# A linear-attention block and two expert layers on one core: a new order of the first four chunks, six early weight halves on TensorE, and later scores

## The chip, the core and the metric

The kernel runs on one core of a Trainium2 chip. The core has five engines that run side by side, each in the order of its own instruction stream: TensorE (PE; its weight loads are shown apart as PEld), VectorE (DVE), ScalarE (ACT), GpSimd (POOL) and SyncE (SP), which here only issues transfers (DMA). SBUF is the on-chip memory, PSUM the memory that TensorE writes its sums to, and HBM the large memory that inputs, outputs and scratch lie in. The metric is device time in microseconds (us) of one execution, from its start to its end.

## The reference, cut

A complex-valued linear recurrence over 768 time steps (4 batches, 8 heads, 48 by 48 states), then a mixture of four experts, then one wide layer with a leaky ReLU:

```python
def _attn_ref(q, k, v, a_re, a_im):
    ...
    for t in range(S):
        new_re = ar * S_re - ai * S_im
        new_im = ar * S_im + ai * S_re
        kv = np.einsum('bhd,bhe->bhde', k[:, :, t], v[:, :, t])
        S_re, S_im = (new_re + kv, new_im)
        y[:, :, t] = np.einsum('bhd,bhde->bhe', q[:, :, t], S_re)

def _moe_ref(x, domain_probs, w1, w2):
    ...
    for e in range(E):
        h = np.maximum(x @ w1[e], 0.0)
        out += p[:, e:e + 1] * (h @ w2[e])

def _moe2_ref(x, w_in, w_out):
    h = x @ w_in
    g = np.maximum(0.01 * h, h)
    return (g @ w_out).astype(np.float32)
```

## The kernel before, in words

The 3072 tokens are cut into 24 chunks of 128, and four chunks make a group of 512. For each chunk there are two pieces of work, both written as generators that are advanced one step (one `yield`) at a time.

`elementwise(c)` turns the four planes of a chunk (real and imaginary decay, q and k) into features. It takes logarithms, exponentials, an arctangent and sines on ACT, running sums and products on DVE (the scans at L202, L207 and L219), range reduction of the phase (L222 to L228), and at last the features `ft` (L243). POOL multiplies q and k by the decay (L208, L215).

`products(c)` does the attention of the chunk. `by_head` (L253) rearranges `ft` into `hd` by six transfers. TensorE transposes the keys (`pt`, L279; ACT copies them to `kt`), forms the scores (`sc`, L292; DVE masks them to `att`), the new state (`pm`, L303) and the output (`py`, L315 and L317; ACT copies it to `y`), and transposes that (`px`, L325). ACT and DVE split `px` into a high part `xh` (L333) and a low part `xl` (L334). These are the inputs of the expert layers. The scores and the output read `hd`; the transposes read only `ft`.

The experts and the wide layer are cut into units of 128 hidden columns, 32 and 16 per group. A unit is nine matmuls of 512 columns into `ph` (L442), a step on DVE and ACT that gives `hp`, `hh` and `hl`, and nine matmuls into the accumulators (L471 to L473). Products run three times, on high and low parts. In group 0 the first eight units are done in halves of 256 columns: first for chunks 0 and 1, then for chunks 2 and 3. In group 0 each expert weight is loaded raw (`load_unit`), split by ACT and POOL into two parts (`split_unit`, L418 and L419), and stored to a scratch in HBM (L608); later uses load the split form (`load_split`, L410). The weights of the wide layer come as 64-bit numbers and are decoded by `decode` from unit 33 on, a third of a half unit at a time (L358 to L368), and stored too (L372).

The order is written out by hand. Ahead of the unit loop the string `PLAN` names what is advanced next: digits are `elementwise` of chunks 0 to 3, the letters p, q, r and t are `products` of chunks 0 to 3, n the probabilities, s one half of a weight to be split. `warm` (L161) adds matmuls that compute nothing that is used. After that `tick` advances one background generator, up to three steps at each of two places per unit, so that a number of steps is done by a given unit (`pace`, L557). For chunks from 4 on, each round of the background has `NSTEPS` steps: those in `PSTEPS` go to `products(c)`, the rest to `elementwise(c + 1)`. With the old table `by_head` is step 1, the transposes are 3 and 5, the scores 8 and 10, the state 13, the output 16 and 18, `px` 21. `load_chunk(c + 2)` stands at the start of the round (L532).

SP issues nearly all transfers in the order of the program, so a transfer that waits holds back those behind it. That matters for three of them: the six `hd` transfers (L261), the loads of chunks (L148, L152), and the loads of raw 64-bit weights (L342), whose buffer is one of three.

Of the kernel before, what the change touches and what calls it, by code (L numbers as in the profile page):

```python
# [20 lines left out]
P = 128  # L21
# [14 lines left out]
WARM = 1, 2, 3, 0  # L36
PLAN = "0100100111100n10s1s0s100s1s0s00110s22113p2q1332p322q32p2p3q2p3q3q2q3p23pq2pq223333"
# [3 lines left out]
FTK = (1,)  # L41
# [7 lines left out]
PSTEPS = (1, 3, 5, 8, 10, 13, 16, 18, 21)  # L49
ESTEPS = 16  # L50
NSTEPS = ESTEPS + len(PSTEPS)
WAIT = 4
HDG = (1,)
# [8 lines left out]
def fused_kernel(  # L62
# [20 lines left out]
    with ExitStack() as fast:  # L83
# [26 lines left out]
        G.memset(ones, 1.0)  # L110
        zero_b = const.tile([P, 1], F32, name="zero_b")
# [49 lines left out]
        def warm(x, n):  # L161

            out = ps_acc.tile([P, TG], F32, name="warm", tag="acc0")
            for _ in range(n):
                PE.matmul(out[:, : NG * P], ident, x.rearrange("p g t -> p (g t)"), start=True, stop=True)

        def elementwise(c):
# [22 lines left out]
            act(r, r, AF.Exp, scale=-1.0)  # L190
# [4 lines left out]
            act(a, a, AF.Ln)  # L195
            S.tensor_tensor(r, en, r, ALU.mult)
            yield
            act(b, a, AF.Exp, scale=-0.5, bias=ln_b)
# [10 lines left out]
            act(a, b, AF.Exp, scale=-0.5)  # L209
# [3 lines left out]
            V.scalar_tensor_tensor(b, en, -1.0, a, ALU.mult, ALU.mult)  # L213
            V.scalar_tensor_tensor(a, b, 2.0, a, ALU.add, ALU.mult)
# [5 lines left out]
            if c >= CPG:  # L220
                yield
# [3 lines left out]
            if c >= CPG:  # L225
                yield
# [3 lines left out]
            if c == 0:  # L230
                warm(th, WARM[0])
# [7 lines left out]
            if c == 1:  # L239
                warm(th, WARM[1])  # L240
            yield
            for i, x in ((0, q), (1, k)):
                (G if i and c in FTK else V).tensor_tensor(  # L243
                    ft[:, :, :, i * P : (i + 1) * P], cs,
                    x[:, None].to_broadcast([P, 2, NG, P]), ALU.mult,
                )
                if i or c >= CPG:
                    yield
# [4 lines left out]
        def by_head(c):  # L253
# [14 lines left out]
        def products(c):  # L268
# [16 lines left out]
            if c < 2:  # L285
                warm(last_phase[c], WARM[2])
# [10 lines left out]
            if c < 2:  # L297
                warm(last_phase[c], WARM[3])
# [49 lines left out]

        def decode(i):
# [18 lines left out]
            G.tensor_tensor(wt[:, 1], wo, wt[:, 0].bitcast(F32), ALU.subtract)  # L368
            yield
            load_raw64(i + 3)  # L370
            if stored:
                SP.dma_start(*stored.pop())  # L372
            stored.append((ws[NU1 + u][:, half], wt.bitcast(F32)))
# [38 lines left out]
        def split_unit(s, part):  # L412
            if s >= len(order) or not fresh[s]:
# [5 lines left out]
            G.tensor_tensor(wt[:, 1], raw, wt[:, 0].bitcast(F32), ALU.subtract)  # L419
            if part:  # L420
# [68 lines left out]
        with tc.manual_schedule():  # L489
# [13 lines left out]
            splits = iter([(0, 0), (0, 1), (1, 0), (1, 1), (2, 0), (2, 1), (3, 0)])  # L503
            for x in PLAN + "0" * 14 + "1" * 14 + "pq" * 8 + "s" * 7:
# [5 lines left out]
                elif x == "s":  # L510
                    for s, part in islice(splits, 1):
                        split_unit(s, part)
                        if part and s < 2:
                            load_unit(s + 5)

            def background():
                for _ in zipped(steps["2"], steps["3"]):
# [307 lines left out]
```

## Time and profile before

| what | value |
|---|---|
| median of 3 runs | 1506.38 us (1501.48 to 2019.27) |
| profiled execution | 1506.07 us, of which its span is 1504.2 us |
| TensorE busy | 1403.8 us, 93% of the span |
| VectorE, ScalarE, GpSimd busy | 864.8, 566.7, 263.6 us |
| chain that ended last | PE 60%, DVE 8%, DMA 3%, ACT 2%, issue 2% |
| HBM | 203 GB/s over the span |

Busy time is the time in which an engine had an instruction under way. "PEclk" is the share of full speed that TensorE's clock was granted in a stretch. It has two levels, 2.4 and 1.2 GHz, so 0.5 is the lower one and a value between them a mix. The number in square brackets behind a row of the timeline is how long the engine stood idle before it, and what released it.

### The profile page before, as it was taken

The numbers are of one execution on the slowest core, as the hardware profiler recorded it, in microseconds if no ns is written. First come the engines' busy times: TensorE is split into PE (matmuls) and PEld (weight loads), VectorE is DVE, ScalarE is ACT, GpSimd is POOL, SyncE is SP. The second block draws the span as 40 slices with busy tenths as digits, with TensorE's granted clock in tenths as the row PEclk, the third lists the DMA queues.
The fourth block names the chain that finished last, engine by engine and source line by source line (L and its number), as shares of the span: only waits on it lengthen the run. The fifth ranks groups of instructions, "written<-read, shape, count | busy, mean of one in ns | idle before, by whom it ended". The sixth has DMA issues, their size and how long they took to land.

```text
span 1504.2 us, 18506 instructions
## 1 busy us (share of the span) xinstructions
PE 1403.8 (93%) x6972; PEld 1177.8 (78%) x6972; DVE 864.8 (57%) x1503; ACT 566.7 (38%) x957; POOL 263.6 (18%) x251
## 2 busy tenths in 40 slices
PE   1888888999899989999999999999999999999997
PEld 0787667888777878878888888888888888888886
DVE  8838566669787878876455555455443333333332
ACT  5535455533444344355333354333242111323232
POOL 5113455311223122121001021001010000100000
PEclk9789989999999999999999999999999999999999
DMA  5498776887788698776776575676565655556562
GB/s 194 53 321 262 243 224 210 246 290 241 236 271 259 248 286 254 264 243 192 236 226 195 195 229 170 232 226 171 178 200 175 218 202 204 193 189 210 190 210 65
DMA packets 91042, 325.48 MB, mean 216 GB/s; under 512 B 10464, under 2 KB 32064, under 8 KB 90944
## 3 DMA queue, kind: packets, MB, share of 16 engines
q1 hardware_dynamic: 88064, 319.24, 66.8%
q10 hardware_dynamic: 2880, 4.98, 1.0%
q8 instruction: 56, 0.92, 0.3%
q14 instruction: 42, 0.34, 0.1%
HBM read 262.72 MB, written 42.52 MB: 203 GB/s over the span
## 4 chain that ended last, share of the span: by engine, by line
PE 60%; DVE 8%; DMA 3%; ACT 2%; issue 2%; POOL 0%; SPq 0%; DVEq 0%; ACTq 0%; POOLq 0%
PE ph L442 27%; PE acc L471 9%; PE acc L473 9%; PE acc L472 9%; DVE hl L460 2%; PE sc L292 1%; PE py L315 1%; PE py L317 1%; DMA vt<-in_v_dram 1%; DVE hp L447 1%; ACT hh L459 1%; DMA ws_scratch<-dw 1%; PE pm L303 1%; DVE ft L243 1%; DMA r<-in_w_dram 1%
## 5 line engine op out<-in xcount | busy, mean ns | idle before, releaser
L442 PE MATMUL ph<-xh,wt 128*128 128x512 f32 (+1 forms) x1200 | 407.5, 396 | 6.9 <-DMA wt<-ws_scratch 6.3
L471 PE MATMUL acc<-hh,wt 128*128 128x512 f32 (+1 forms) x888 | 350.0, 394 | 6.9 <-ACT o L586 6.9
L473 PE MATMUL acc<-hl,wt 128*128 128x512 f32 (+1 forms) x888 | 341.9, 385 | 0.0
L472 PE MATMUL acc<-hh,wt 128*128 128x512 f32 (+1 forms) x888 | 341.2, 384 | 0.0
L459 ACT CAST hh<-hp 128x512 fp32r<-128x512 f32 (+1 forms) x296 | 180.6, 610 | 402.1 <-DVE hp L447 315.4
L460 DVE TENSOR_TENSOR hl<-hp,hh 128x512 fp32r<-128x512 f32 (+1 forms) x296 | 213.5, 721 | 183.6 <-ACT hh L459 183.1
L442 PEld LDWEIGHTS ph<-xh,wt 128*128 128x128 f32 x1200 | 231.4, 195 | 51.8 <-DMA wt<-ws_scratch 7.4
L447 DVE SCALAR_TENSOR_TENSOR hp<-ph,pb 128x512 f32<-128x512 f32 (+1 forms) x200 | 133.4, 667 | 199.9 <-PE ph L442 199.8
L442 PE MATMUL ph<-xl,wt 128*128 128x512 f32 (+1 forms) x600 | 234.5, 391 | 1.1 <-DVE xl L334 1.1
L442 PE MATMUL ph<-x2h,wt 128*128 128x512 f32 x576 | 198.0, 398 | 0.0
L471 PEld LDWEIGHTS acc<-hh,wt 128*128 128x128 f32 x888 | 167.5, 189 | 38.2 <-ACT o L586 7.6
L473 PEld LDWEIGHTS acc<-hl,wt 128*128 128x128 f32 x888 | 167.1, 188 | 34.1
L472 PEld LDWEIGHTS acc<-hh,wt 128*128 128x128 f32 x888 | 167.7, 189 | 31.0
L450 DVE SCALAR_TENSOR_TENSOR hp<-hp 128x512 f32<-128x512 f32 x96 | 72.3, 753 | 171.7 <-ACT hp L449 171.7
L442 PEld LDWEIGHTS ph<-xl,wt 128*128 128x128 f32 x600 | 117.4, 196 | 22.0 <-DVE xl L334 1.6
L442 PEld LDWEIGHTS ph<-x2h,wt 128*128 128x128 f32 x576 | 108.7, 189 | 25.2
L449 ACT COPY hp<-ph 128x512 f32<-128x512 f32 x96 | 56.3, 586 | 168.0 <-PE ph L442 168.0
L442 PE MATMUL ph<-x2l,wt 128*128 128x512 f32 x288 | 114.5, 397 | 0.0
L292 PE MATMUL sc<-hd 96*128 96x128 f32 x384 | 58.3, 302 | 35.8 <-DMA hd<-ft 26.7
L292 PEld LDWEIGHTS sc<-hd 96*128 96x128 f32 x384 | 55.7, 215 | 42.8 <-issue 22.7
L419 POOL TENSOR_TENSOR wt<-raw,wt 128x384 fp32r<-128x384 f32 x64 | 71.9, 1144 | 57.2 <-ACT wt L418 56.9
L208 POOL TENSOR_TENSOR aaqk<-aaqk,ge 128x384 f32<-128x384 f32 x24 | 26.5, 1103 | 252.1 <-DVE ge L207 252.1
(94 smaller groups left out, 1467.2 us busy)
## 6 DMA issues: line engine op xcount, KB each, us to landing
wt<-ws_scratch SPq DMA_DIRECT2D x264, 768.0 KB, 4.8
ws_scratch<-wt SPq DMA_DIRECT2D x32, 768.0 KB, 8.1
hd<-ft SPq DMA_DIRECT2D x142, 128.5 KB, 7.2
aaqk<-in_attn_dram SPq DMA_DIRECT2D x22, 768.0 KB, 5.8
raw<-in_w_dram SPq DMA_DIRECT2D x32, 384.0 KB, 4.1
r<-in_w_dram SPq DMA_DIRECT2D x32, 384.0 KB, 3.8
ws_scratch<-dw SPq DMA_DIRECT2D x32, 384.0 KB, 4.2
pb<-pn_scratch SPq DMA_DIRECT2D x24, 256.0 KB, 6.5
```

The lines of the kernel that those rows point to most:

```text
L208: G.tensor_tensor(q, q, en, ALU.mult)
L292: PE.matmul(sc[:, j], hd[:, h, P : 2 * P], hd[:, h, :P], start=True, stop=True)
L419: G.tensor_tensor(wt[:, 1], raw, wt[:, 0].bitcast(F32), ALU.subtract)
L442: PE.matmul(ph[:, : t1 - t0], wt[:, wi, cols], x[kc][:, t0:t1], start=n == 0, stop=n == 3 * NG - 1)
L447: V.scalar_tensor_tensor(hp, ph, 0.0, pbs[g, u // 8][:, t0:t1], ALU.max, ALU.mult)
L449: A.copy(hp, ph)
L450: V.scalar_tensor_tensor(hp, hp, 0.01, hp, ALU.mult, ALU.max)
L459: A.copy(hh, hp)
L460: V.tensor_tensor(hl, hp, hh.bitcast(F32), ALU.subtract)
L471: PE.matmul(out, wt[:, 0, cols], hh, start=first, stop=False)
L472: PE.matmul(out, wt[:, 1, cols], hh, start=False, stop=False)
L473: PE.matmul(out, wt[:, 0, cols], hl, start=False, stop=last)
```

## The change

It has five parts.

1. **Order of the start.** A new `PLAN` finishes the features of chunks 0 and 1, then their products, and takes chunks 2 and 3 only eight steps far ahead of the unit loop (14 before), the rest in the background. The `warm` matmuls go. The features of chunk 1 are all made by DVE (POOL made half of them). Three of the six `hd` transfers of chunks 0 and 1 are issued by ACT.
2. **Early weight halves.** Six halves are split by a new way: ACT casts the high part (`cast_early`), TensorE forms the rest as raw minus high in PSUM with the identity and its negative, and ACT copies it out (`rest_early`). POOL has no part in it.
3. **Steps of `elementwise`.** ACT takes the square first and the exponential of r later; one exponential goes to `g` in place of `a`; there are 17 steps for all chunks.
4. **Later scores.** The scores move from steps 8 and 10 to 12 and 14 of a round, what follows moves by four steps or three, and `load_chunk(c + 2)` moves from the start of the round to step 9.
5. **Decoding.** The store of the decoded half is issued ahead of the next raw load, and that load goes to the buffer freed one half earlier.

```diff
-WARM = 1, 2, 3, 0
-PLAN = "0100100111100n10s1s0s100s1s0s00110s22113p2q1332p322q32p2p3q2p3q3q2q3p23pq2pq223333"
+PLAN = (
+    "0101001010101011" "01ss0000mm" "00sss11mm000" "1111ppsm23111qq"
+    "23232n3pp23p2ppqq3q23qqpq23m"
+)
-FTK = (1,)
-PSTEPS = (1, 3, 5, 8, 10, 13, 16, 18, 21)
-ESTEPS = 16
+PSTEPS = (1, 3, 5, 12, 14, 17, 20, 22, 24)
+ESTEPS = 17
+LOADSTEP = 9
...
+        minus = const.tile([P, P], F32, name="minus")
+        A.mul(minus, ident, -1.0)
...
-            act(r, g, AF.Ln)
-            act(a, g, AF.Square)
...
+            act(a, g, AF.Square)
+            act(r, g, AF.Ln)
...
-            act(a, b, AF.Exp, scale=-0.5)
+            act(g, b, AF.Exp, scale=-0.5)
...
-                (G if i and c in FTK else V).tensor_tensor(
+                V.tensor_tensor(
...
-                    (A if c in HDG and i == ri else SP).dma_start(hd[row : row + DG], ft[:, ri, i])
+                    (A if c < 2 and (i == ri or i == 2 - ri) else SP).dma_start(hd[row : row + DG], ft[:, ri, i])
...
-            if c < 2:
-                warm(last_phase[c], WARM[2])
...
+        def store_decoded(left):
+            while len(stored) > left:
+                SP.dma_start(*stored.pop(0))
...
-            yield
-            load_raw64(i + 3)
-            if stored:
-                SP.dma_start(*stored.pop())
             stored.append((ws[NU1 + u][:, half], wt.bitcast(F32)))
+            yield
+            store_decoded(1)
+            if i:
+                load_raw64(i + 2)
...
+        early_cast, early_done = [], set()
+        def cast_early(s, part):
+
+            if s not in wts:
+                wts[s] = p_w.tile([P, 2, 2, DM], F32R, name="wt", bufs=WTS)
+            A.copy(wts[s][:, part, 0], raws[s][:, part])
+            early_cast.append((s, part))
+        def rest_early():
+
+            if not early_cast:
+                return
+            s, part = early_cast.pop(0)
+            raw, wt = raws[s][:, part], wts[s][:, part]
+            rest = ps_h.tile([P, TG], F32, name="ph")[:, :DM]
+            PE.matmul(rest, ident, raw, start=True, stop=False)
+            PE.matmul(rest, minus, wt[:, 0].bitcast(F32), start=False, stop=True)
+            A.copy(wt[:, 1], rest)
+            early_done.add((s, part))
...
                 for c in range(CPG, NCHUNK):
-                    if c + 2 < NCHUNK:
-                        load_chunk(c + 2)
                     todo = products(c)
                     ahead = elementwise(c + 1) if c + 1 < NCHUNK else iter(())
                     for k in range(NSTEPS):
+                        if k == LOADSTEP and c + 2 < NCHUNK:
+                            load_chunk(c + 2)
                         next(todo if k in PSTEPS else ahead, None)
                         yield
```

**VectorE at the first `xl`.** Before, on VectorE, this stands just ahead of the `xl` of chunks 0 and 1 (`th` and `ge` are the phase of chunk 3; the same block for chunk 2 stands right above it):

```order
L213 SCALAR_TENSOR_TENSOR tb<-ge,ta 128x384
L214 SCALAR_TENSOR_TENSOR ta<-tb,ta 128x384
L234 COPY ft<-ge 128x6
L219 SCALAR_TENSOR_TENSOR th<-ones,th,tr 128x128 x3
L222 TENSOR_SCALAR ge<-th 128x384
L223 TENSOR_SCALAR ge<-ge 128x384
L224 TENSOR_TENSOR th<-th,ge 128x384
L227 TENSOR_SCALAR th<-th 128x384
L228 TENSOR_SCALAR ge<-th 128x384
L334 TENSOR_TENSOR xl<-px,xh 128x3x128 x2
```

Of the changed kernel, on VectorE, the same `xl` (now L320) and its neighbours, where L196 and L198 are the first running sum of chunk 3, and L203 the running products of chunks 2 and 3:

```order
L281 TENSOR_TENSOR att<-sc,causal 128x512 x2
L196 SCALAR_TENSOR_TENSOR ta<-ta,tb 128x384
L198 SCALAR_TENSOR_TENSOR tb<-ones,ta 128x128 x3
L295 TENSOR_TENSOR st<-pm,st 96x384
L296 TENSOR_TENSOR st<-st,hd 96x384
L320 TENSOR_TENSOR xl<-px,xh 128x3x128 x2
L203 SCALAR_TENSOR_TENSOR ge<-ta,ones 128x128 x6
L460 SCALAR_TENSOR_TENSOR hp<-ph,pb 128x256
```

The running products, the phases and the range reduction of chunks 2 and 3 moved from ahead of the first `xl` to behind it.

**SyncE at chunk 5.** Before, the queue of SyncE around the six `hd` transfers of chunk 5 (`aaqk` and `vt` are the load of chunk 7):

```order
L402 DMA raw<-in_w_dram 128x768
L148 DMA aaqk<-in_attn_dram 128x1536
L152 DMA vt<-in_v_dram 128x384
L261 DMA hd<-ft 16x8x257 x6
L608 DMA ws_scratch<-wt 128x1536
```

Of the changed kernel, the same place:

```order
L392 DMA raw<-in_w_dram 128x768
L251 DMA hd<-ft 16x8x257 x6
L626 DMA ws_scratch<-wt 128x1536
L392 DMA raw<-in_w_dram 128x768
L626 DMA ws_scratch<-wt 128x1536
L150 DMA aaqk<-in_attn_dram 128x1536
L154 DMA vt<-in_v_dram 128x384
```

The chunk load moved from ahead of the `hd` transfers to behind them, past two stores and a raw load.

**TensorE at chunk 5.** Before, on TensorE, from the last transposes of chunk 5 to its first scores:

```order
L279 MATMUL pt<-ident,ft 128x128 x3
L471 MATMUL acc_550<-hh,wt 128x512
L472 MATMUL acc_550<-hh,wt 128x512
L473 MATMUL acc_550<-hl,wt 128x512
L471 MATMUL acc_551<-hh,wt 128x512
L472 MATMUL acc_551<-hh,wt 128x512
L473 MATMUL acc_551<-hl,wt 128x512
L471 MATMUL acc_552<-hh,wt 128x512
L472 MATMUL acc_552<-hh,wt 128x512
L473 MATMUL acc_552<-hl,wt 128x512
L292 MATMUL sc<-hd 128x128 x4
```

Of the changed kernel, the end of the same stretch; ahead of these rows stand the last transposes (now six in one row), nine matmuls of `ph` and eight of `acc`:

```order
L486 MATMUL acc_508<-hl,wt 128x512
L455 MATMUL ph<-xh,wt 128x512
L455 MATMUL ph<-xl,wt 128x512
L455 MATMUL ph<-xh,wt 128x512 x2
L455 MATMUL ph<-xl,wt 128x512
L455 MATMUL ph<-xh,wt 128x512 x2
L455 MATMUL ph<-xl,wt 128x512
L455 MATMUL ph<-xh,wt 128x512
L280 MATMUL sc<-hd 128x128 x4
```

Between the last transposes and the scores stand 27 large matmuls in place of 9. Counted in the same way it is 45 in place of 18 for chunk 4, 27 in place of 18 for chunks 6 and 7, and 36 in place of 18 for chunks 9, 10 and 11.

## Rows read from the trace of the kernel before

**Rows 1.** Windows: us, then busy us (instructions) by engine, PEclk, DMA share, GB/s.

```profile
0.00:65.90 65.90, 27.73 (x148) 21.07 (x148) 57.57 (x109) 37.22 (x60) 25.93 (x32) 0.90 0.49 131
65.90:109.70 43.80, 38.35 (x273) 37.50 (x273) 17.97 (x35) 12.88 (x28) 9.05 (x9) 0.80 0.94 260
109.70:330.00 220.30, 194.24 (x1060) 167.09 (x1060) 144.66 (x257) 105.58 (x187) 86.58 (x79) 0.94 0.78 248
330.00:700.00 370.00, 348.49 (x1734) 291.16 (x1734) 298.43 (x547) 159.39 (x271) 87.91 (x80) 0.97 0.78 252
700.00:1504.00 804.00, 794.98 (x3760) 660.98 (x3759) 346.21 (x557) 251.65 (x412) 54.09 (x51) 1.00 0.61 196
```

**Rows 2.** Waits of TensorE: who waited for what, us in total, times, longest.

```profile
PE sc L292 <- DMA hd<-ft: 26.7, 7, 7.1
...
PE sc L292 <- ACT hh L459: 6.3, 1, 6.3
...
PE ph L442 <- DMA wt<-ws_scratch: 6.3, 5, 2.2
```

**Rows 3.** Timeline, TensorE waiting for scores: start, us, instruction, idle before.

```profile
181.18 2.05 PE L292 MATMUL sc<-hd 96*128 96x128 f32 x8 [6.95 <-DMA hd<-ft]
...
221.81 2.05 PE L292 MATMUL sc<-hd 96*128 96x128 f32 x8 [7.15 <-DMA hd<-ft]
...
384.97 2.04 PE L292 MATMUL sc<-hd 96*128 96x128 f32 x8 [6.31 <-ACT hh L459]
```

**Rows 4.** Windows of ten us after two of these waits.

```profile
180.00:190.00 10.00, 8.82 (x40) 7.72 (x41) 3.49 (x7) 1.04 (x2) 0.00 (x0) 0.70 0.65 268
220.00:230.00 10.00, 8.19 (x34) 7.12 (x35) 4.55 (x10) 1.24 (x2) 0.00 (x0) 0.65 0.76 303
```

**Rows 5.** Timeline of the queue of SyncE at chunk 5: start, us, transfer.

```profile
168.63 0.38 SPq L148 DMA_DIRECT2D aaqk<-in_attn_dram  x1
169.10 0.38 SPq L152 DMA_DIRECT2D vt<-in_v_dram  x1
169.58 4.02 SPq L261 DMA_DIRECT2D hd<-ft  x6
```

**Rows 6.** Landing of `hd`, from 165 to 195 us.

```profile
DMA to landing us min/median/max: 7.9/8.6/8.7
```

**Rows 7.** Landing of `hd`, from 30 to 80 us (no chunk load ahead of them).

```profile
DMA to landing us min/median/max: 3.3/5.2/8.1
```

**Rows 8.** The chain, in order of time: nine large matmuls in a stream.

```profile
712.74 2.04 PE ph L442 x9
```

**Rows 9.** Timeline of VectorE, start of the kernel: phases of chunks 0 and 2, the `xl`.

```profile
21.66 3.34 DVE L219 TENSOR_TENSOR_SCAN th<-ones,tr 128x128 f32<-128x128 f32 x3
...
58.11 1.22 DVE L219 TENSOR_TENSOR_SCAN th<-ones,th,tr 128x128 f32<-128x128 f32 x3
...
66.57 1.01 DVE L334 TENSOR_TENSOR xl<-px,xh 128x384 fp32r<-128x384 f32 x2
...
109.11 0.56 DVE L334 TENSOR_TENSOR xl<-px,xh 128x384 fp32r<-128x384 f32 x1 [0.42 <-ACT xh L333]
```

**Rows 10.** Timeline of TensorE, end of the first products and first unit.

```profile
56.88 0.39 PE L315 MATMUL py<-vt,att 128*128 128x48 f32 x2
...
61.12 0.63 PE L315 MATMUL py<-vt,att 128*128 128x48 f32 x2
...
65.92 0.58 PE L442 MATMUL ph<-xh,wt 128*128 128x256 f32 x1 [0.57 <-ACT xh L333]
```

**Rows 11.** Waits of the queue of SyncE over the whole span.

```profile
SPq L342 <- DVE d L363: 161.5, 22, 9.9
```

**Rows 12.** Timeline of TensorE and ScalarE at the output of chunk 12.

```profile
501.86 0.98 PE L315 MATMUL py<-vt,att 128*128 128x48 f32 x8
...
508.25 0.52 ACT L367 CAST dw<-d 128x384 fp32r<-128x384 f32 x1 [4.83 <-DVE d L366]
...
508.67 0.47 ACT L321 COPY y<-py 128x384 f32<-128x384 f32 x1
```

More of the change, by code (lines that the diff above doesn't have):

```diff
@@ L2 @@
 from contextlib import ExitStack
-from itertools import islice
 import concourse.bass as bass
@@ L159, in table @@
                 tables[0] = name
[L161 to L165, printed above, removed]
         def elementwise(c):
@@ L189, in elementwise @@
             T.tensor_tensor(a, a, b, ALU.add)
-            act(r, r, AF.Exp, scale=-1.0)
+            yield
+            act(a, a, AF.Ln)
             V.scalar_tensor_tensor(
@@ L194, in elementwise @@
             yield
-            act(a, a, AF.Ln)
+            act(b, a, AF.Exp, scale=-0.5, bias=ln_b)
+            act(r, r, AF.Exp, scale=-1.0)
             S.tensor_tensor(r, en, r, ALU.mult)
-            yield
-            act(b, a, AF.Exp, scale=-0.5, bias=ln_b)
             yield
@@ L212, in elementwise @@
             act(r, r, AF.Arctan)
-            V.scalar_tensor_tensor(b, en, -1.0, a, ALU.mult, ALU.mult)
-            V.scalar_tensor_tensor(a, b, 2.0, a, ALU.add, ALU.mult)
+            yield
+            V.scalar_tensor_tensor(b, en, -1.0, g, ALU.mult, ALU.mult)
+            V.scalar_tensor_tensor(a, b, 2.0, g, ALU.add, ALU.mult)
             G.tensor_tensor(k, k, a, ALU.mult)
@@ L229, in elementwise @@
             last_phase[c] = th
-            if c == 0:
-                warm(th, WARM[0])
             yield
@@ L246, in elementwise @@
                 )
-                if i or c >= CPG:
-                    yield
+                yield
             feats[c] = (ft, vt)
@@ L296, in products @@
                 yield
-            if c < 2:
-                warm(last_phase[c], WARM[3])
             old = state.pop(c, None)
@@ L368, in decode @@
             G.tensor_tensor(wt[:, 1], wo, wt[:, 0].bitcast(F32), ALU.subtract)
+            stored.append((ws[NU1 + u][:, half], wt.bitcast(F32)))
             yield
-            load_raw64(i + 3)
-            if stored:
-                SP.dma_start(*stored.pop())
-            stored.append((ws[NU1 + u][:, half], wt.bitcast(F32)))
+            store_decoded(1)
+            if i:
+                load_raw64(i + 2)
         whole, halves = (0, TG), ((0, TG // 2), (TG // 2, TG))
@@ L412, in split_unit @@
         def split_unit(s, part):
-            if s >= len(order) or not fresh[s]:
+            if s >= len(order) or not fresh[s] or (s, part) in early_done:
                 return
@@ L419, in split_unit @@
             G.tensor_tensor(wt[:, 1], raw, wt[:, 0].bitcast(F32), ALU.subtract)
+            if part:
+                del raws[s]
+        early_cast, early_done = [], set()
[14 more added lines that the diff above has]
+            early_done.add((s, part))
             if part:
@@ L502, in fused_kernel @@
             steps.update(zip("pqrt", (products(c) for c in range(CPG))))
-            splits = iter([(0, 0), (0, 1), (1, 0), (1, 1), (2, 0), (2, 1), (3, 0)])
-            for x in PLAN + "0" * 14 + "1" * 14 + "pq" * 8 + "s" * 7:
+            early_halves = iter([(s, part) for s in range(6) for part in (0, 1)][: PLAN.count("s")])
+            for x in PLAN + "m" * 8:
                 if x in steps:
@@ L510, in fused_kernel @@
                 elif x == "s":
[L511 to L514, printed above, removed]
+                    cast_early(*next(early_halves))
+                elif x == "m":
+                    rest_early()
+            for s in (5, 6):
+                load_unit(s)
+            split_unit(3, 0)
             def background():
+                for _ in range(2):
+                    next(steps["2"])
+                    yield
                 for _ in zipped(steps["2"], steps["3"]):
@@ L551, in decoding @@
                 yield
-                SP.dma_start(*stored.pop())
+                store_decoded(0)
             dec = decoding()
-            first = max(0, 14 - min(PLAN.count("2"), PLAN.count("3"))) + WAIT + E2 - PLAN.count("r") - PLAN.count("t")
+            first = 2 + max(0, ESTEPS + 1 - min(PLAN.count("2"), PLAN.count("3"))) + WAIT + E2 - PLAN.count("r") - PLAN.count("t")
             pace = [(0.0, 0), (KN, first)]
```

9 lines of the change are left out of this document (2 added, 7 removed).

## The prediction, and how it is worked out

> **What bounds the kernel now.** I read the windows by stretch first, to see where TensorE is not busy or not at full clock [rows 1]. From 700 us on it is busy for 794.98 of 804 us at full clock, so nothing there can be gained but the little tail. The loss lies ahead of that, in three stretches. Up to 65.9 us TensorE is busy for 27.73 us, and VectorE for 57.57: the start is a chain through VectorE. From 65.9 to 109.7 us the clock is 0.80. From 109.7 to 700 us TensorE stands idle for 26.1 + 21.5 = 47.6 us, and the clock, 0.94 and 0.97, costs about 0.06 x 194 + 0.03 x 348 = 22 us more.
>
> Then I read who TensorE waits for [rows 2]. Scores that wait for `hd` are 26.7 us in seven waits. One more of 6.3 us is put down to ScalarE's `hh`, but it, too, stands ahead of scores [rows 3], in a round of the same build. So scores cost 33.0 us of idle time in eight waits. Each long one is followed by a stretch at the lower clock: 0.70 and 0.65 in the ten us after 180 and 220 us [rows 4], which is 0.30 x 8.82 = 2.6 us and 0.35 x 8.19 = 2.9 us. The reader is to see that a wait of 7 us is worth about 9.5.
>
> Why `hd` is late is seen in SyncE's queue and in the landings. For chunk 5 the load of chunk 7 goes out at 168.63 us, and the six `hd` transfers behind it from 169.58 to 173.6 us [rows 5]. They land after 8.6 us each [rows 6], so at 181 to 182 us, when the scores start. In the start, with no chunk load ahead, the median is 5.2 us [rows 7].
>
> **The later scores.** The order shows 18 more large matmuls between transposes and scores for chunks 5 and 9 to 11, 9 more for chunks 6 to 8, 27 more for chunk 4. A large matmul in a stream takes 2.04 / 9 = 0.227 us [rows 8], so scores come 4.1, 2.0 and 6.1 us later in TensorE's own work. The chunk load that no longer stands ahead gives 169.58 - 168.63 = 0.95 us of queue [rows 5], and of the landing between nothing and 8.6 - 5.2 = 3.4 us [rows 6, 7]. I take 2.5, nearer the upper end, because the two landings differ mainly in what stands ahead. Set against the waits [rows 3]: chunk 5, 6.95 - 4.1 - 0.95 - 2.5, below zero; chunk 6, 7.15 - 2.0 - 0.95 - 2.5 = 1.7 left; chunk 10, 6.31 - 4.1 - 0.95 - 2.5, below zero. One of the eight waits is in the start and counts there; of the other 32 us I take 28 as saved. With no gain in the landing, chunk 5 keeps 1.9 and chunk 6 keeps 4.2, so about 24 is the lower bound.
>
> With the waits go their low-clock stretches. Of the 22 us above I take 13, two at 2.6 to 2.9 as in rows 4 and five or so of somewhat less [rows 4]; the rest follows other waits. Bounds: 5.5 (those two alone) and 22.
>
> The moved chunk load is itself late by nothing: at step 9 its buffers have been free since the round before, and the features that need it start 18 steps later. At 26 + 1 steps a round and some 40 us a round (from 181.18 to 221.81 us [rows 3]) that is 27 us, against a landing of the order of rows 6. If that cover were gone, VectorE's features would slip, and the next `hd` with them.
>
> **The decoding.** SyncE waits 161.5 us, in 22 waits, for VectorE to free a raw buffer [rows 11], and the weights behind it in the queue arrive late: TensorE waits 6.3 us for `wt` in five waits [rows 2]. The load now goes to a buffer freed one half earlier. Not all five lie in the decoding, so I take 3 us (bounds 0 and 6.3).
>
> **What it costs.** `px` now stands nearer to `py`: counted in the order, 18 large matmuls in place of 27 in the rounds of chunks 13 to 15, which is 4.1 us in place of 6.1 [rows 8]. ScalarE's `y` must come in between. In the decoding it can be late: the output of chunk 12 ends at 502.84 us and `y` starts at 508.67, because a decoded half ahead of it in ScalarE's queue waits for VectorE [rows 12]. That is 5.8 us, so 1.7 us would be left uncovered; in seven chunks of the decoding (9 to 15) at most 12 us. I take 4, since decoding is also what SyncE's queue relieves, and 0 to 12 as bounds.
>
> **The start.** The first unit needs `xl`, written at 66.57 us, right behind a block of VectorE work on chunks 2 and 3 that runs without a gap from 58.11 us [rows 9]. The order puts that block behind `xl`: 8.5 us. The early halves take six POOL operations out of the time in which VectorE is stretched: the first three scans take 3.34 us there and 1.22 later [rows 9]. I take 4 us for that, between 0 and 8 (four times the 2.1 us of those scans). So `xl` comes at about 66.6 - 8.5 - 4 = 54 us. Bounds: 66.6 - 8.5 - 8 = 50; and 66.6 - 8.5 + 5.2 = 63, if POOL's relief is worth nothing and the three `hd` transfers of each chunk that now go out on ScalarE's queue, among its copies, land later by as much as one takes [rows 7]. The twelve new matmuls, six copies and casts lie on TensorE and ScalarE, busy for 27.73 and 37.22 of 65.9 us [rows 1].
>
> But the first unit is not the end of the start. The second half of these units needs `xl` of chunk 3, at 109.11 us, which is 42.5 us after the first [rows 9]. What moved behind the first lengthens that distance: by at least nothing and at most 8.5 us. TensorE's queue is in order and soon waits for chunk 2, so I take 3.5: 54 + 46 = 100 in place of 109, a gain of 9. Bounds: 50 + 42.5 gives 17, 63 + 51 loses 5.
>
> The missing `warm` matmuls are weighed here. With them, a pair of output matmuls took 0.39 us at 56.88 us and 0.63 at 61.12 [rows 10], so they held the higher clock for a while and not to the first unit. The Trainium skill, "TensorE: Matmul & The Clock Gate", section "What's actually happening", has it that the low clock is the default and that activity releases it, so the first products without warm-up would run at 1.2 GHz. The trace agrees that a quiet stretch is followed by the low clock [rows 4]. What it would do here is a rival below.
>
> **The sum.** 28 + 13 + 3 - 4 + 9 = 49 us off the profiled execution's own 1506.1 us gives 1457. The median of the three runs shown, 1506.4, is the same within 0.3 us.
>
> **The rivals.**
>
> *The start gains nothing.* If the products of chunks 0 and 1 run at the lower clock, some 10 us of TensorE's work ahead of `xl` (of the 27.73 in that stretch [rows 1]) take 0.63 / 0.39 = 1.6 times as long [rows 10], up to 6 us more on the path, and the later `xl` of chunk 3 slips with it. Then the start gains 0 to 3: 1463 to 1466, say 1465. For it speaks that TensorE does little before; against it, that the following wait for chunk 2 hides low-clock units.
>
> *The transfers become the bound in group 0.* From 109.7 to 330 us the engines' DMA share is 0.78 at 248 GB/s [rows 1]. The same bytes in 220 - 30 us would be 0.90. Then `hd` lands later again, and half of that stretch's gain stays away: about 15 us, 1472. By the limit of 358 GB/s in the Trainium skill, "DMA: Bandwidth & Descriptors", section "Specifications", the 290 GB/s of the shorter stretch would still fit.
>
> *Slower: `y` behind the decoding.* VectorE is busy for 298 of 370 us there [rows 1]; with the stalls gone its queue is fuller. If the lag of `y` doubles to 11.6 us, 7.5 us are uncovered in each of seven chunks, and each is followed by some 2.7 us of low clock [rows 4]: 7 x 10.2 = 71 in place of 4, 1457 + 67 = 1524. It outweighs the gain from a lag of about 9 us on. Against it: `y` lags so far only where a decoded half stands ahead.
>
> *More.* All terms at their better bounds: 32 + 22 + 6 - 0 + 17 = 77, 1429; half-way to it, 1442.
>
> **How the numbers follow.** Chances: the forecast 0.60 (1446 to 1470), transfers 0.14, no gain in the start 0.10, more 0.13, slower 0.03. Predicted is 1457. The range 1438 to 1480 leaves out the slower case, the far end of more and a worse case of the transfers, under 2 in 10. Two per cent, about what a measurement of this kernel can tell from no change, is 30 us, so 1476 is the border. Under it lie nearly all of the forecast, of more and of the start, and six in ten of the transfers: 0.87. Same is 0.10, slower by over 2% 0.03.
>
> **What would show it.** Of the scores' waits in 109.7 to 700 us less than 5 us is left, and the clock there is 0.98 or more. The first `ph` starts near 54 us, and the fourth `xl` is written near 100. SyncE's wait for raw 64-bit weights has gone. If `hd` still ends the waits after 150 us, the landing was not the chunk load's; if `px` waits for `y`, the slower rival is at work.

## The result, and the profile after

The changed kernel takes 1480.23 us, the median of four executions (1477.27 to 1483.39), against 1505.77 us of the kernel before. The ratio is 0.984, with a 95% interval of 0.9804 to 0.9876; one execution of the kernel before that took 2019.27 us is left out of it. It is faster by 25 us where 49 were forecast. That is less than the 2% to which the forecast gave 0.87, and the time lies just above the end of the range. The profiled execution took 1478.36 us, with a span of 1476.6.

The windows of the changed kernel, with the columns of [rows 1]:

```profile
0.00:65.90 65.90, 37.68 (x152) 30.70 (x153) 41.33 (x87) 31.23 (x56) 10.16 (x20) 0.75 0.49 125
65.90:109.70 43.80, 27.12 (x170) 25.73 (x169) 27.20 (x50) 13.87 (x30) 14.10 (x13) 0.73 0.68 174
109.70:330.00 220.30, 211.29 (x1216) 182.52 (x1216) 167.51 (x282) 116.90 (x207) 93.62 (x84) 0.99 0.87 281
330.00:700.00 370.00, 358.85 (x1810) 299.77 (x1809) 308.54 (x558) 166.21 (x281) 91.22 (x80) 1.00 0.79 265
```

From 109.7 to 700 us the forecast came true: TensorE is idle for 9.0 + 11.2 = 20 us in place of 47.6, and the clock is 0.99 and 1.00 in place of 0.94 and 0.97. But the stretch from 65.9 to 109.7 us has become worse: busy 27.12 us in place of 38.35, at 0.73 in place of 0.80. The start didn't gain, it lost.

Waits of TensorE from 109.7 to 700 us:

```profile
PE px L311 <- ACT y L307: 5.8, 4, 2.4
...
PE sc L280 <- DMA hd<-ft: 1.5, 2, 1.1
...
PE sc L280 <- ACT ge L121: 0.8, 1, 0.8
```

The scores (L280 now, L292 before) wait 1.5 us for `hd`, where the three waits of [rows 3] alone were 20 us (one of them put down to `hh`). In their place stand waits of `px` for `y`, 5.8 us, of the kind that the forecast priced at 4.

Waits of TensorE up to 109.7 us, and VectorE's `xl` in the start:

```profile
PE pt L269 <- DVE ft L234: 13.7, 3, 9.4
...
PE sc L280 <- DMA hd<-ft: 5.4, 1, 5.4
```

```profile
64.74 0.56 DVE L320 TENSOR_TENSOR xl<-px,xh 128x384 fp32r<-128x384 f32 x1 [6.86 <-ACT xh L319]
...
66.03 2.77 DVE L203 TENSOR_TENSOR_SCAN ge<-ta,ones 128x128 f32<-128x128 f32 x6
...
84.83 0.95 DVE L234 TENSOR_TENSOR ft<-cs,aaqk 128x768 f32<-128x768 f32 x1
...
123.10 0.56 DVE L320 TENSOR_TENSOR xl<-px,xh 128x384 fp32r<-128x384 f32 x1 [2.92 <-ACT xh L319]
```

The first `xl` is written at 64.74 us (66.57 before, 54 forecast), the fourth at 123.10 (109.11 before, 100 forecast [rows 9]). Between them TensorE's transposes wait 9.4 us at a stretch for VectorE's features `ft` of chunks 2 and 3, the first of which start only at 84.83 us, and then the scores wait 5.4 us for `hd`.

So the sum failed mainly in one place, the start. The experiments first cut the change in two, then take each half apart.

### The profile page after: what moved, and what is told of

Its sections match the earlier page's. It is cut to its first block, busy times and chain, and to the rows that moved or that the text cites. A ratio compares the mean times of both kernels' runs of the same rounds, so it can differ in the third digit from the quotient of the medians.

```text
span 1476.6 us, 18540 instructions
## 1 busy us (share of the span) xinstructions
PE 1402.4 (95%) x6978; PEld 1177.2 (80%) x6978; DVE 864.7 (59%) x1504; ACT 564.8 (38%) x961; POOL 264.5 (18%) x244
## 4 chain that ended last, share of the span: by engine, by line
PE 58%; DVE 2%; ACT 0%; issue 0%; DVEq 0%; ACTq 0%
PE ph L455 27%; PE acc L484 9%; PE acc L486 9%; PE acc L485 9%; PE sc L280 1%; PE py L301 1%; PE py L303 1%; PE pm L289 1%; PE pt L269 0%; DVE hl L473 0%; DVE hp L460 0%; PE px L311 0%; DVE d L349 0%; ACT hh L472 0%; DVE d L355 0%
## 5 line engine op out<-in xcount | busy, mean ns | idle before, releaser
L455 PE MATMUL ph<-xh,wt 128*128 128x512 f32 (+1 forms) x1200 | 397.9, 388 | 0.0
L455 PEld LDWEIGHTS ph<-xh,wt 128*128 128x128 f32 x1200 | 225.5, 190 | 42.4 <-ACT ge L121 0.3
L455 PE MATMUL ph<-xl,wt 128*128 128x512 f32 (+1 forms) x600 | 230.2, 384 | 0.0
L455 PEld LDWEIGHTS ph<-xl,wt 128*128 128x128 f32 x600 | 114.1, 190 | 20.3 <-DVE xl L320 0.2
L409 POOL TENSOR_TENSOR wt<-raw,wt 128x384 fp32r<-128x384 f32 x58 | 65.0, 1142 | 62.4 <-ACT wt L408 62.3
L643 POOL TENSOR_TENSOR x2l<-o,x2h 128x512 fp32r<-128x512 f32 x18 | 25.2, 1424 | 256.4 <-ACT x2h L642 256.4
L301 PE MATMUL py<-vt,att 128*128 128x48 f32 x384 | 70.9, 280 | 0.1
L280 PEld LDWEIGHTS sc<-hd 96*128 96x128 f32 x384 | 54.2, 208 | 15.4 <-issue 7.9
```

The costliest lines, as they stand in the source:

```text
L280: PE.matmul(sc[:, j], hd[:, h, P : 2 * P], hd[:, h, :P], start=True, stop=True)
L301: PE.matmul(py[:, h], att[:, h], vt[:, h * D : (h + 1) * D], start=True, stop=first)
L455: PE.matmul(ph[:, : t1 - t0], wt[:, wi, cols], x[kc][:, t0:t1], start=n == 0, stop=n == 3 * NG - 1)
```

## Experiments: the change cut in two

**mid_only** keeps the start of the kernel before, with its own elementwise function for chunks 0 to 3, and takes the rest of the change:

```diff
-PSTEPS = (1, 3, 5, 8, 10, 13, 16, 18, 21)
-ESTEPS = 16
+PSTEPS = (1, 3, 5, 12, 14, 17, 20, 22, 24)
+ESTEPS = 17
+LOADSTEP = 9
...
-            steps = {str(c): elementwise(c) for c in range(CPG)}
+            steps = {str(c): elementwise0(c) for c in range(CPG)}
```

> The kernel before with its own start (plan, warm matmuls, low halves by POOL, transfers), and with the change only from chunk 4 on: elementwise in 17 steps, later scores, chunk load at step 9, the new order in the decoding. Theory A (the two parts add up; the middle gained what was forecast and the start lost 14 us): 1506 - 41 = 1465 us, first xl at about 66.6 and fourth at about 109 us as before, waits for hd under 8 us in all. Rival B (the middle gains because the changed start delays or spreads the transfers): about 1480 us or more, with hd waits of 5 us or more left after 150 us.

**start_only** is the other half: the changed plan, early halves, transfers and elementwise work of chunks 0 to 3, and from chunk 4 on everything as before. Against the changed kernel:

```diff
-PSTEPS = (1, 3, 5, 12, 14, 17, 20, 22, 24)
-ESTEPS = 17
-LOADSTEP = 9
+PSTEPS = (1, 3, 5, 8, 10, 13, 16, 18, 21)
+ESTEPS = 16
+LOADSTEP = 0
...
-                store_decoded(0)
+                SP.dma_start(*stored.pop())
```

> The changed kernel's start alone; from chunk 4 on features, steps, chunk load and decoding as in the kernel before. Theory A (parts add up): 1506 + 14 = 1520 us, fourth xl near 123 us as in the changed kernel. Rival C (a late start is made good by waits for hd that shrink with it): about 1506 us.

Measured: mid_only 1470.53 us, ratio 0.9781 (0.9749 to 0.9813); start_only 1534.84 us, ratio 1.0203 (1.0171 to 1.0235), both against 1504.88. So the middle alone gains 34 us, more than the whole change and nearer to theory A (1465 us) than to rival B (1480 or more), and the start alone loses 30, which neither of its two expectations (1520 and 1506 us) foresaw. That the start loses is shown; that the parts add up isn't: with the new middle the start costs 1480.2 - 1470.5 = 10 us, with the old one 30. Waits of TensorE in both, from 109.7 to 700 us:

```profile
PE sc L373 <- ACT ge L120: 4.4, 1, 4.4
...
PE sc L373 <- DMA hd<-ft: 0.5, 1, 0.5
```

```profile
PE sc L362 <- DMA hd<-ft: 35.7, 8, 10.1
```

With the old middle the late start makes the scores wait 35.7 us for `hd`, in eight waits of up to 10.1 us; in the kernel before it was 25.8 us in six. These 10 us more are not yet the 30 that are lost, and the rest was not taken apart.

## Experiments: the terms of the middle

Three kernels each put one edit of mid_only back.

```diff
mid_noscore
-PSTEPS = (1, 3, 5, 12, 14, 17, 20, 22, 24)
+PSTEPS = (1, 3, 5, 8, 10, 13, 16, 18, 21)
mid_noload
-LOADSTEP = 9
+LOADSTEP = 0
mid_nodec
...
-            store_decoded(1)
-            if i:
-                load_raw64(i + 2)
+            load_raw64(i + 3)
+            if stored:
+                SP.dma_start(*stored.pop())
...
```

> mid_only (1470.5 us) with the scores back at steps 8 and 10 and what follows them at its old steps; chunk load at step 9, elementwise in 17 steps and the decoding's new order stay. Theory A (the later scores are the main term: by the forecast 4.1, 2.0 and 6.1 us of cover for chunks 5, 6 and 10, with the clock behind them): waits for hd or put down to scores come back to 15 us or more, time 1485 to 1495 us. Rival H (the chunk load that stands ahead of hd in SyncE's queue was the cause of nearly all): waits under 6 us, time 1470 to 1476 us.

> mid_only (1470.5 us) with the chunk load back at the start of the round, ahead of the hd transfers; the later scores stay. Theory A (forecast: 0.95 us of queue and 2.5 of landing a chunk, so that waits of about 2.9 at chunk 5 and 5.2 at chunk 6 stay): 8 to 10 us of waits for hd come back and the time is 1478 to 1484 us. Rival H (the chunk load is the whole cause): waits of 20 us or more, 1495 us. Rival I (the later scores cover it alone): within 3 us of 1470.5.

> mid_only (1470.5 us) with the decoding's old order: raw load of half i + 3 behind half i, and the store behind it. Forecast: the new order was worth about 3 us, so 1473 to 1474 us, with SyncE's wait for raw 64-bit buffers back to about 150 us and waits for wt 3 us longer. Rival J (SyncE's wait is idle time of no use to anyone): within 2 us of 1470.5. Rival K (the old order also delays hd and wt of the stretch from 330 to 700 us): 1478 us or more.

Measured, all against 1503.97 us: mid_noscore 1492.68 (ratio 0.9934, 0.9914 to 0.9954), mid_noload 1479.12 (0.9844, 0.9818 to 0.9869), mid_nodec 1471.09 (0.9789, 0.9772 to 0.9806). The later scores are worth 22 us, the moved chunk load 8.6, the decoding's order 0.6, which is nothing that these runs can tell. TensorE's scores that wait for `hd` (start, us, instruction, idle before) in mid_noload and mid_noscore:

```profile
175.76 1.13 PE L373 MATMUL sc<-hd 96*128 96x128 f32 x8 [3.48 <-DMA hd<-ft]
...
211.25 2.04 PE L373 MATMUL sc<-hd 96*128 96x128 f32 x8 [4.75 <-DMA hd<-ft]
```

```profile
172.67 1.19 PE L373 MATMUL sc<-hd 96*128 96x128 f32 x8 [2.57 <-DMA hd<-ft]
...
212.35 2.04 PE L373 MATMUL sc<-hd 96*128 96x128 f32 x8 [6.21 <-DMA hd<-ft]
```

With the load ahead of `hd` again, chunks 5 and 6 wait 3.48 and 4.75 us; the forecast's account of these chunks leaves 6.95 - 4.1 = 2.9 and 7.15 - 2.0 = 5.2 for the load. With early scores chunk 5 waits 2.57 us in place of 6.95, so the load alone takes 4.4 off, where 3.45 was forecast; but chunk 6 waits 6.21 in place of 7.15, and there it takes off only 0.9. The landing shows the load more plainly. DMA issues from 110 to 330 us (tile, queue, KB each, median us to landing), mid_noload and mid_only, which differ by the load alone:

```profile
hd<-ft SPq DMA_DIRECT2D x36, 128.5 KB, 7.8
```

```profile
hd<-ft SPq DMA_DIRECT2D x36, 128.5 KB, 5.3
```

That is 2.5 us earlier, as taken from [rows 6, 7]. The Trainium skill, "DMA: Bandwidth & Descriptors", section "Issuing engines are not separate DMA queues", says that transfers end up on the same 16 engines and interleave, whoever issues them. Load and `hd` are both issued by SyncE here, so these runs show of it only that the load in front of `hd` delays its landing, and not only its issue.

For the decoding, waits of SyncE's queue in mid_nodec and mid_only:

```profile
SPq L423 <- DVE d L444: 170.0, 23, 12.2
```

```profile
SPq L432 <- POOL dw L453: 86.2, 19, 11.2
```

The wait for raw buffers (170.0 us, of the kind in [rows 11]) goes, and one of the store for `dw` (86.2) comes. As the time is the same, neither is on the path that sets it.

## Experiments: why the start loses

Three suspects: the low clock of the first products, VectorE's work that now stands behind the first `xl`, and the early halves on TensorE.

**The clock.** Windows of TensorE in the changed kernel, then in the kernel before:

```profile
45.00:50.00 5.00, 5.00 (x29) 5.00 (x29) 3.02 (x8) 0.00 (x0) 0.00 (x0) 0.50 0.38 134
...
55.00:60.00 5.00, 5.00 (x28) 5.00 (x27) 2.58 (x6) 0.62 (x1) 0.00 (x0) 0.50 0.00 0
60.00:65.00 5.00, 5.00 (x24) 4.70 (x24) 0.26 (x1) 0.96 (x2) 0.00 (x0) 0.50 0.00 0
```

```profile
55.00:60.00 5.00, 4.97 (x48) 4.97 (x48) 4.85 (x11) 2.85 (x4) 1.59 (x2) 0.97 0.02 5
60.00:65.00 5.00, 5.00 (x25) 4.65 (x24) 4.79 (x12) 3.01 (x6) 1.18 (x1) 0.50 0.00 0
```

From 45 to 65 us (of the four windows three are shown) TensorE does products of chunks 0 and 1 without a gap, at 0.50. after_warm puts matmuls back into its gaps (`warm` as in the kernel before):

```diff
+            if c < 2:
+                warm(last_phase[c], 3)
             att = pool.tile([P, H, P], F32, name="att", bufs=1)
...
+            if c == 0:
+                warm(last_phase[c], 6)
             old = state.pop(c, None)
```

> The changed kernel with matmuls put back that fill TensorE's gaps: 3 ahead of the scores of chunks 0 and 1, 6 between scores and state of chunk 0. Theory D (the start lost by the low clock from 44 to 65 us): granted clock near 1.00 from about 46 us on, first xl near 56 us in place of 64.7, fourth near 113, time about 1480 - 10 = 1470 us. Rival E (VectorE's work on chunks 2 and 3 that now stands behind xl decides): first xl earlier, but the fourth within 4 us of 123, time 1476 to 1480. Rival F (the products do not hold the clock whatever ran ahead of them): clock 0.50 again, xl near 66, time 1480 or 2 us more.

**VectorE's order.** after_order changes the plan alone, so that two more steps of chunks 2 and 3 (the scans of `en`, ScalarE's exp, table load and arctan) stand ahead of the first `xl`; after_order3 has some more (about 6.8 us of VectorE):

```diff
-    "23232n3pp23p2ppqq3q23qqpq23m"
+    "23232n3pp23p2ppqq3q232323qqpq23m"
...
+    "23232n3pp23p2ppqq3q2323232223qqpq23m"
```

> The changed kernel with two more steps of chunks 2 and 3 (the scans of en, the exp, table load and arctan) ahead of the last half of chunk 1's products, in the 6.9 us in which VectorE waits for xh. Theory E (VectorE's work behind xl decides): the fourth xl comes 3 to 6 us earlier than 123, time about 1475 us. Theory D (the clock alone): first xl at 65 to 66 as before, the fourth 0 to 2 us earlier, time within 2 us of 1480.

> The changed kernel with five more steps of chunk 2 and three more of chunk 3 ahead of the last half of chunk 1's products (about 6.8 us more of VectorE's work ahead of the first xl than in after_order). Theory E (VectorE's work on chunks 2 and 3 that stands behind the first xl decides the fourth): first xl up to 3 us later than 64.8, fourth xl 4 to 7 us earlier than 118.0, time 1466 to 1470 us. Rival G (first units held up cost as much as they give): fourth xl earlier, but time 1473 or more.

Measured: after_warm 1475.66 us (1469.84 to 1480.05; ratio 0.9801, 0.9765 to 0.9837), after_order 1472.83 (0.9797, 0.9767 to 0.9827), after_order3 1469.16 (0.9768, 0.9749 to 0.9787). The clock and the `xl` of after_warm:

```profile
45.00:50.00 5.00, 5.00 (x29) 5.00 (x29) 3.03 (x8) 0.00 (x0) 0.00 (x0) 0.50 0.42 132
...
55.00:60.00 5.00, 5.00 (x50) 4.92 (x49) 3.90 (x8) 0.61 (x1) 0.00 (x0) 1.00 0.00 0
60.00:65.00 5.00, 4.95 (x26) 3.65 (x24) 1.96 (x5) 2.46 (x5) 0.00 (x0) 0.66 0.00 0
```

```profile
62.64 0.56 DVE L331 TENSOR_TENSOR xl<-px,xh 128x384 fp32r<-128x384 f32 x1 [2.77 <-ACT xh L330]
...
124.44 0.56 DVE L331 TENSOR_TENSOR xl<-px,xh 128x384 fp32r<-128x384 f32 x1 [2.92 <-ACT xh L330]
```

Of these 20 us the clock is wholly up from 55 to 60 us only, the first `xl` comes 2.1 us earlier, and the fourth doesn't come earlier than the 123.10 of the changed kernel. (Its median is 4.6 us under that of the changed kernel, but the executions of the two overlap, so that isn't told from no change.) The `xl` of after_order and after_order3:

```profile
64.81 0.56 DVE L320 TENSOR_TENSOR xl<-px,xh 128x384 fp32r<-128x384 f32 x1 [4.20 <-ACT xh L319]
...
118.00 0.56 DVE L320 TENSOR_TENSOR xl<-px,xh 128x384 fp32r<-128x384 f32 x1 [0.73 <-ACT xh L319]
```

```profile
65.49 1.01 DVE L320 TENSOR_TENSOR xl<-px,xh 128x384 fp32r<-128x384 f32 x2
...
113.29 0.56 DVE L320 TENSOR_TENSOR xl<-px,xh 128x384 fp32r<-128x384 f32 x1 [0.41 <-ACT xh L319]
```

Here the first `xl` comes no earlier (64.81 and 65.49 us), at the same low clock from 45 to 65 us, and the fourth comes 5 and then 10 us earlier; the kernel is 7 and 11 us faster than the changed one, and after_order3 is as fast as mid_only. So with the low clock of the first products and the early halves left as they are, the order of VectorE's work alone wins back these 10 us.

**The early halves and the block.** after_pool takes the early low halves off TensorE; before_block is the kernel before, with the block of VectorE work that ran from 58.11 to 66.57 us [rows 9] put behind the first `xl`:

```diff
after_pool
-            early_cast.append((s, part))
...
+            G.tensor_tensor(wt[:, 1], raw, wt[:, 0].bitcast(F32), ALU.subtract)
+            early_done.add((s, part))
...
before_block (end of the plan)
-q2p3q3q2q3p23pq2pq223333
+q2p3q3qqppqpq22232323333
```

> The changed kernel with the six early low halves by POOL again, in place of twelve matmuls and six copies, at the same steps of the plan. The forecast's step (POOL's six operations in the start cost VectorE 4 us at the first xl): first xl near 69 us in place of 64.7, fourth near 127, time 1484 us. Rival N (VectorE's relief is taken up by waits for TensorE and ScalarE): first xl within 1 us of 64.7 and time within 3 us of 1480.

> The kernel before with one change: the phase steps of chunks 2 and 3 (scans of th, range steps, 8.5 us of VectorE from 58.1 to 66.6 us) stand behind the first two xl, and ScalarE's table loads and sines of them behind xh; TensorE's order is the same. The forecast's step (that block holds the first xl): first xl near 58 us, fourth xl 109 us or less, time about 1500 us. Theory M (xl also waits for xh, which TensorE's products give only at 65 to 66 us): first xl at 64.5 to 66, no more than 2 us earlier; fourth xl 6 to 9 us later, at 115 to 118; time 1510 to 1526 us.

Measured: after_pool 1485.69 us (0.987, 0.9838 to 0.9902); before_block 1506.08 (1.0018, 0.9996 to 1.0039). VectorE in after_pool, and the first scans of `th` in the changed kernel:

```profile
18.16 3.34 DVE L216 TENSOR_TENSOR_SCAN th<-ones,tr 128x128 f32<-128x128 f32 x3
...
68.40 0.56 DVE L320 TENSOR_TENSOR xl<-px,xh 128x384 fp32r<-128x384 f32 x1 [6.86 <-ACT xh L319]
```

```profile
18.27 1.79 DVE L216 TENSOR_TENSOR_SCAN th<-ones,tr 128x128 f32<-128x128 f32 x3
```

So POOL's six subtractions cost VectorE 68.40 - 64.74 = 3.7 us at the first `xl`, about the 4 of the forecast. At the first unit it is 2.5 us (69.23 and 66.74 us), as in the changed kernel the last of the early halves stand ahead of the unit in TensorE's queue. The median is 5.5 us higher, but the executions of the two overlap, so the worth for the whole kernel isn't told from nothing; the early halves on TensorE, the third suspect, aren't what makes the start lose, since the kernel is no faster without them. The Trainium skill, "Trainium Architecture — The Big Picture", section "What this means for kernel authors", says that VectorE and GpSimd contend for a shared pair of ports by an exclusive lock; the scans, 3.34 us with POOL at work and 1.79 without, agree.

VectorE in before_block, and ScalarE's `xh` in the kernel before:

```profile
63.77 0.56 DVE L334 TENSOR_TENSOR xl<-px,xh 128x384 fp32r<-128x384 f32 x1 [5.66 <-ACT xh L333]
...
76.30 1.83 DVE L243 TENSOR_TENSOR ft<-cs,aaqk 128x768 f32<-128x768 f32 x2 [0.78 <-ACT cs L119]
...
109.33 0.56 DVE L334 TENSOR_TENSOR xl<-px,xh 128x384 fp32r<-128x384 f32 x1 [0.42 <-ACT xh L333]
```

```profile
64.81 1.06 ACT L333 CAST xh<-px 128x384 fp32r<-128x384 f32 x2
```

With 8.5 us taken from ahead of it, `xl` comes 2.8 us earlier, and waits 5.66 us for `xh`. The fourth `xl` stays at 109.33, though chunk 3's features start only at 76.30, so theory M was right in its first half and wrong in its second. What the first `xl` gains is lost right behind it: the block now stands ahead of the first unit's `hp`, which comes at 78.04 us in place of 71.05, and TensorE waits 9.2 us for the `hh` made of it. That chunk 3's features can come 7 us later without harm is likely slack, not tested by itself: chunk 3's products stand behind those of chunk 2 in TensorE's queue.

## Experiments: what was left open between the halves

That the start costs 10 or 30 us leaves open which part of the middle takes it up. Three kernels put one part back in the changed kernel: the early scores, the early chunk load, and the elementwise work of chunks 4 on in its 16 steps and their old order.

```diff
after_noscore
-PSTEPS = (1, 3, 5, 12, 14, 17, 20, 22, 24)
+PSTEPS = (1, 3, 5, 8, 10, 13, 16, 18, 21)
after_noload
-LOADSTEP = 9
+LOADSTEP = 0
after_el16
-ESTEPS = 17
+ESTEPS = 16
...
```

> The changed kernel with the scores back at steps 8 and 10 and what follows at its old steps; its start, chunk load at step 9 and decoding stay. Theory A (start and scores add up): 1480 + 22 = 1502 us, with about 16 us of waits for hd. Theory L (a start that ends 14 us later brings features and scores of chunks 5 to 8 closer together, so that early scores wait longer): 25 us or more of waits for hd, 1508 to 1520 us.

> The changed kernel with the chunk load back at the start of the round, ahead of the hd transfers; start, later scores and decoding stay. If the parts add up: +8.6 as between mid_noload and mid_only, 1488 to 1490 us, with about 10 us of waits for hd. If the chunk load is what makes the changed start dear with the old middle (start_only lost 30 us, the changed kernel against mid_only 10): 1500 us or more, with 20 us or more of waits for hd.

> The changed kernel with the elementwise work of chunks 4 on in the old 16 steps and their old order; start, later scores, chunk load at step 9 and decoding stay. If the parts add up: the 17 steps are worth what is left of the middle's 34.4 us after 22.2, 8.6 and 0.6, that is 3 us, so about 1483 us. If the order of ScalarE's work in these steps is what the changed start needs: 1495 us or more, with waits that end at ScalarE or VectorE ahead of scores.

Measured: after_noscore 1493.45 us (0.9933, 0.9909 to 0.9957), after_noload 1507.09 (1.0015, 1.0000 to 1.0029), after_el16 1497.69 (0.9957, 0.9941 to 0.9972). With the new start the later scores are worth 13 us in place of 22, the moved chunk load 27 in place of 8.6, and the 17 steps 17 in place of the 3 that the old start leaves for them (a remainder, not a run). Together that is 58 us, near the 55 between start_only and the changed kernel. The 13 us of the later scores fit neither theory of after_noscore. Waits of TensorE in after_noload from 109.7 to 700 us, then its windows:

```profile
PE sc L280 <- DMA hd<-ft: 8.8, 2, 4.9
PE ph L455 <- DMA wt<-ws_scratch: 8.2, 2, 5.0
```

```profile
109.70:330.00 220.30, 201.52 (x1126) 174.84 (x1125) 145.40 (x252) 107.24 (x191) 89.22 (x80) 0.93 0.81 260
330.00:700.00 370.00, 355.29 (x1787) 297.22 (x1786) 309.69 (x561) 161.66 (x276) 90.02 (x80) 0.98 0.78 257
```

They show more waits for `wt` (8.2 us in two) than mid_noload has (5.9 in seven), and about as many for `hd` (8.8 and 8.6); the 20 us of `hd` waits that were expected with a time over 1500 us didn't come. But the windows show a second road. TensorE is idle for 18.8 + 14.7 = 33.5 us in place of 20.2, which is 13 more, and the clock is 0.93 and 0.98 in place of 0.99 and 1.00: in windows of ten us, busy time multiplied by what the clock lacks of full speed adds up to some 18 us in place of 3. The two together are 28 of the 34 us between the two profiled executions (that of after_noload, 1512.27 us, is the slowest of its ten). In after_noscore and after_el16, too, the clock costs more (10 and 12 us) than the idle time that is added (5 and 4; in after_el16 it is mostly `pm` that waits for VectorE's `att`, 10.1 us), while in mid_noload it is 7 us of idle time and 1 of clock against mid_only. So with the late start more than half of the loss in these stretches is low clock. Why the same edits bring so much more of it there isn't settled.

## Why the prediction was wrong, point by point

**The middle was right and a little large.** Forecast 28 + 13 + 3 - 4 = 40; mid_only gained 34. Scores and load, with their clock, were 41 in the forecast and are 22 + 8.6 = 31, if they add up. The 3 us for the decoding were wrong: SyncE's long wait held nothing that TensorE needed. The sign of less than 5 us of score waits in the middle came true: 1.5 for `hd` and 0.8 for ScalarE's `ge` are the largest left.

**The step that failed is "the start", in two of its terms**, the block at the first `xl` and the distance to the fourth: +9 forecast and -10 measured.

*The block of 8.5 us at the first `xl`.* The forecast took it that VectorE's block ended the wait, as `xl` stands right behind it [rows 9]. But `xl` also needs `xh`, which ScalarE wrote from 64.81 to 65.87 us; the row on which this could be seen stood in the forecast itself: the first unit at 65.92 waits for `xh`, not for `xl` [rows 10]. Two inputs came within a microsecond of each other, and taking one away gave 2.8 us, not 8.5. What the block cost TensorE stands in the trace of the kernel before, one row behind those of [rows 10]: the first matmul that reads `xl` waits 1.14 us for it (2.21 in mid_noload, whose start is the same).

```profile
67.64 0.58 PE L442 MATMUL ph<-xl,wt 128*128 128x256 f32 x1 [1.14 <-DVE xl L334]
```

Against 66.6 - 2.8 - 3.7 = 60.1 us, the measured 64.7 is 4.6 late. Two things can be the cause. One is the low clock of the products; after_warm had back 2.1 us of it. The other is again VectorE's order: in the changed kernel the scores of chunk 0 end at 40.26 us, but VectorE takes the probabilities and steps of chunks 2 and 3 before it masks them, so that TensorE waits 4.2 us:

```profile
44.47 2.79 PE L289 MATMUL pm<-vt,kt 128*96 128x48 f32 x16 [4.21 <-DVE att L281]
```

No run moves that work, so how the 4.6 us divide stays open.

*The distance from the first to the fourth `xl`.* It was bounded at 42.5 + 8.5 = 51 and is 123.10 - 64.74 = 58.4 (62.5 to 62.7 in the four other profiles of this start). The forecast counted the one block that it knew. Between the first two `xl` and the features at 84.83 us VectorE has scans and range steps of chunks 2 and 3 for some 16 us (its rows from 66.03 on, without the units' own `hp` and `hl`). The scans of `ge` among them stood at 48.88 and 55.65 us before. So `hd` of these chunks goes out 17 us later. VectorE in the kernel before, then SyncE's queue before and after:

```profile
48.88 1.06 DVE L207 TENSOR_TENSOR_SCAN ge<-ta,ones 128x128 f32<-128x128 f32 x3
```

```profile
69.39 7.75 SPq L261 DMA_DIRECT2D hd<-ft  x12
```

```profile
86.75 7.71 SPq L251 DMA_DIRECT2D hd<-ft  x12
```

The 8 us of before_block were hidden at the fourth `xl`; 17 were not. after_order and after_order3 showed it by moving such steps back.

*The clock* was priced as a rival, up to 6 us and the fourth `xl` with it. The products at the lower clock take some 20 us (44.47 to 65 us), where the forecast had 10 x 1.6 = 16. But the 2.1 us that after_warm gains at the first `xl` don't reach the fourth, and after_order3 wins 10 us there with the products' clock as low as before. The clock from 100 us on does move the fourth `xl`, by 4 us between executions (last section).

*What was right in the start:* POOL's relief, 4 us forecast and 3.7 measured. The size is partly luck: the forecast took the first three scans to lose 3.34 - 1.22 = 2.1 us, and they lose 3.34 - 1.79 = 1.55.

**The rivals.** Transfers as a bound did not come (DMA share 0.87 at 281 GB/s from 109.7 to 330 us, and scores don't wait). `y` behind the decoding is 5.8 us of waits, within its bounds. The rival on the start had the right place, with a gain of 0 to 3 as its worst; a loss of 10 stood outside even the term's bounds, 17 and -5, and with a middle that is a little short it puts the time at the end of the range.

## What to carry to other kernels

When a block of work is moved from ahead of an instruction, look up when its other inputs come: the gain ends at the second latest. List every row that changes sides, add up its times, and follow the sum to the next transfer that it feeds, not to the next instruction. A transfer that stands in a queue ahead of one that is waited for is worth moving, and the worth depends on how late the rest is: 9 us here with an early start, 27 with a late one.

## What the runs showed of the hardware

From 45 to 65 us of the changed kernel TensorE was busy for 5.00 of 5.00 us in four windows in a row, and stayed at the granted clock 0.50, the lower level of 1.2 GHz; in the kernel before it fell from 0.97 to 0.50 in the middle of such products, without a gap. The Trainium skill, "TensorE: Matmul & The Clock Gate", section "What's actually happening", has it that activity releases the low clock; these 20 us of products didn't.

The column of the granted clock can mislead in a start. In after_pool its row from 0 to 65.9 us says 1.00, but the output products there take as long as at 0.50 in the changed kernel (0.63 us a pair; 0.39 at the higher level [rows 10]):

```profile
60.16 0.63 PE L301 MATMUL py<-vt,att 128*128 128x48 f32 x2
```

So the low clock of the products doesn't come from the early halves: after_pool has it without them. The column falls below 1.00 only from 85 us on in that trace. That it says 1.00 until the first change that a trace holds is likely, and not shown; the time of a known matmul tells the clock either way.

The same start isn't the same in each execution. Windows of the changed kernel, and of after_noload, whose program is the same up to there:

```profile
100.00:105.00 5.00, 5.00 (x32) 5.00 (x31) 1.63 (x4) 0.00 (x0) 0.00 (x0) 0.58 1.04 340
...
110.00:115.00 5.00, 4.43 (x35) 4.20 (x34) 1.71 (x4) 1.75 (x4) 1.00 (x1) 0.89 1.00 419
```

```profile
100.00:105.00 5.00, 5.00 (x30) 5.00 (x29) 2.14 (x4) 0.00 (x0) 0.00 (x0) 0.50 1.06 286
...
110.00:115.00 5.00, 4.43 (x22) 4.27 (x22) 0.59 (x2) 1.37 (x3) 0.99 (x1) 0.50 1.02 425
```

In one execution the clock rises from 100 us on, in the other not before 115, with about the same busy time, and the fourth `xl` comes at 123.10 and 127.34 us. The profiles of start_only, after_noscore and after_el16 have the later one too (127.24 to 127.36), so that 123.10 is the lucky execution of five. Differences of 4 us between single profiles of this start tell nothing; the 5 and 10 us of after_order and after_order3 are beyond that, the 1.3 of after_warm is not.
